# Two leading steps of a recurrent-attention and FFN kernel, regrouped as one batch with 256 tokens in 64-row tiles

## The chip, the cores and the metric

The kernel runs on one core of one Trainium2 chip. A core has engines that run side by side: TensorE (PE, matmuls; PEld is its weight load), VectorE (DVE), ScalarE (ACT), GpSimd (POOL) and SyncE (SP), and 16 DMA engines that all of them share. Each engine works through its own list of instructions in order; semaphores hold one engine back for another. The metric is device time in microseconds of the whole program, lower is better. The profile is of one execution on the chip.

## What is computed

A gated linear recurrence over 768 tokens (4 batches, 8 heads of 48), and after it a feed-forward network with a ReLU gate over all 3072 token rows:

```python
f = 1.0 / (1.0 + np.exp(-f_logit))
for t in range(S):
    state = f[:, :, t, :, None] * state + np.einsum('bhd,bhe->bhde', k[:, :, t], v[:, :, t])
    y[:, :, t] = np.einsum('bhd,bhde->bhe', q[:, :, t], state)
x = y.transpose(0, 2, 1, 3).reshape(B * S, H * D)          # 3072 x 384
gate = np.maximum(x @ w_gate, 0.0)                         # 384 x 1536
out = (gate * (x @ w_val)) @ w_out                         # 1536 x 384
```

## The kernel before

Time is cut into six steps of 128 tokens; a step takes all four batches, so 512 token rows. For a step, the attention makes a block `xT` (three times 128 features by 512 rows), and the FFN works on that block.

Attention of one batch in one step: f is turned into minus the log of the gate (ACT: Exp, then Ln, to `bneg`); a matmul with a triangle of ones sums it over the tokens ("cum"); ACT takes exponentials of both signs; k and q times these are the "hats" (`hats`); both are transposed to `qkT`; scores are k-hats by q-hats, one matmul for each head; DVE multiplies them by a triangular mask into `ptm`; the "rows" matmuls (`ps<-ptm,vpad` and `ps<-qkT,st`) add `ptm` times v and q-hats times the state to y; k-hats times v ("state", `ps<-vpad,hats`) go to the new state (`new_state`: one product in step 0, else a sum on DVE to `ssum` and a product on POOL to `st`). v is spread to `vpad` by POOL.

Three ways of transposing are in use. In steps 1 and 2 PE transposes the hats and DVE copies them (`pe_hats`, lines 687 to 700). From step 3 on the crossbar of the DMA does it (line 702, issued by SP). y comes out of PE already transposed where `x_way` is "tiled" (steps 0 to 2, 32-column tiles); else it comes out in natural order (lines 763 to 773) and the crossbar transposes it (line 795).

Step 0 is special (`twos = (0,)`, `attention_pair`). Two batches are taken together: each partition holds two neighbouring tokens of one batch, partitions 0 to 63 one batch and 64 to 127 the other, so that a DMA packet of f, k and q has two tokens, 384 bytes, instead of one token's 192. v is loaded in the plain way. The sum over tokens then needs two matrices (`upto`, `below`), and the transposes are written interleaved so that tokens come in order. As k-hats in token order are needed once more for the state, four more transposes a batch and a copy bring them back (`attention_back`, lines 623 to 637).

FFN (`ffn_hidden`, `ffn_out`): for each of 12 slices j of the hidden dimension, three matmuls for the gate (line 834), ReLU on ACT (840), three for the value (834 too), product on DVE to `gT` (844); then 12 matmuls for each batch with `wo` (877), ACT copies (887), SP stores (891). For a part of the slices, given by `halves`, the matmuls of two batches (256 columns) are done apart, so that the FFN can start with half of a block.

The order of work is not written by hand. Each operation is given to a planner (`Plan`) with an engine, an estimated duration and a priority; it lays all engines' lists out, picks PSUM banks by groups with limits, and puts in the semaphore waits. Written by hand is the order of the first DMAs, the string `first`: items run in this order on SP (inputs) and on POOL (weights: "wg0", "wv0" are thirds of the two first matrices); what follows an "@" is a load that must have landed first. In `link`, an operation named both in `after` (such a gate) and in `follows` (the predecessor in the same chain) keeps the second kind, which sets only the order.

```python
first = ("f0.0 k0.0 q0.0 v0.0 f0.1 k0.1 q0.1 v0.1 wg0@f0.1 wv0 wg1@q0.1 wv1 wg2 wv2 f1.0@wv1 k1.0 q1.0 v1.0 wo0@q1.0 wo1 wo2 "
         "f1.1 k1.1 q1.1 v1.1").split()
```

"f1.0" is f of step 1, first pair of batches. Until 15 us of the plan, PE is fed matmuls of zeros (lines 929 and 938) in its gaps.

Of the kernel before, what the change touches and what calls it, by code (L numbers as in the profile page):

```python
# [299 lines left out]
def bass_hgrn2_outer__then__ffn_reglu_kernel(  # L300
# [10 lines left out]
    twos = (0,)  # L311
    pe_hats = {(1, 0), (1, 1), (2, 0), (2, 1)}
    halves = {0: 6, 1: 6, 2: 6}
    x_way = {(c, pr): "tiled" if c < 3 else "xbar" for c in range(6) for pr in range(2)}
    s_twin = {(c, pr) for c in range(6) for pr in range(2)} - {(0, 0), (1, 0)}
    y_twin = {(1, 1), (2, 0), (2, 1)}
    flight = 3
    wsteps = 3
    first = ("f0.0 k0.0 q0.0 v0.0 f0.1 k0.1 q0.1 v0.1 wg0@f0.1 wv0 wg1@q0.1 wv1 wg2 wv2 f1.0@wv1 k1.0 q1.0 v1.0 wo0@q1.0 wo1 wo2 "
             "f1.1 k1.1 q1.1 v1.1").split()  # L320
# [32 lines left out]
    dec = [sb(f"dec{i}", [128, B, NP, 2], F32) for i in range(NA)]  # L353
# [20 lines left out]
    pick2 = sb("pick2", [128, 2], BF16)  # L374
    ident = sb("ident", [128, 128], BF16)
# [4 lines left out]
    pl = Plan({"bc": 2, "bc4": 4, "tp": 2, "s": 4, "y": 2, "kv": 1, "f": 4})  # L380
# [28 lines left out]
    def triangle(t, name, base, prio):  # L409
# [9 lines left out]
                                         pattern=[[0, 64], [1, 2]], channel_multiplier=-1), ["pick"], ["pick"], occ=0.3, prio=-20)  # L419
# [10 lines left out]
    add("DVE", lambda: ve.tensor_copy(pick2[:], same.ap[:, 0:2]), [same], ["pick2"], occ=0.1, prio=-19)  # L430
# [8 lines left out]
    for i in range(NA):  # L439
        fill("DVE", f"dec{i}", dec[i][:], 0.0, 32, -14)  # L440
# [20 lines left out]
    def load(n, c, b0, b1, after=()):  # L461
        last = tails.get("load")
        t = ld[n]
        both = c in twos and n != "v"
        if both:
            src = bass.AP(tensor=srcs[n].tensor, offset=b0 * H * S * D + c * C * D,
                          ap=[[2 * D, C // 2], [S * D, 2 * H], [1, 2 * D]])
            dst = bass.AP(tensor=t, offset=slot_of(n, c, b0 // 2) * 2 * HD, ap=[[NL[n] * 2 * HD, 128], [2 * D, H], [1, 2 * D]])
        else:
            src = bass.AP(tensor=srcs[n].tensor, offset=b0 * H * S * D + c * C * D,  # L470
                          ap=[[D, C], [S * D, (b1 - b0) * H], [1, D]])
            dst = t[:, slot_of(n, c, b0 // 2), :, :, :].rearrange("p b h d -> p (b h) d")
        op = add("SP", lambda: sy.dma_start(dst, src), [], in_keys(n, c, b0, b1),  # L473
                 occ=0.7 if both else 1.0, lat=0.9, prio=c * 100, after=after,
                 follows=[last] if last else [])
        tails["load"] = op
        dma(op, f"{n}{slot_of(n, c, b0 // 2)}", 0.95 * (b1 - b0), (64, 19, 27) if both else (128, 13.5, 23))
# [21 lines left out]
    loads, done = [], {}  # L499
    for item in first:  # L500
        item, _, behind = item.partition("@")
        gate = [done[behind]] if behind else []
        if item[0] == "w":
            op = load_w(item[:2], int(item[2:]), gate)
        else:
            c, pr = (int(x) for x in item[1:].split("."))
            op = load(item[0], c, 2 * pr, 2 * pr + 2, gate)
        done[item] = op
        if item[0] != "w":
            loads.append(op)  # L510

    def chain(line, *args, **kw):

        last = tails.get(line)
        tails[line] = add(*args, follows=[last] if last else [], **kw)
        return tails[line]
# [10 lines left out]
    def tokens(c, b, x, p, lo=0, hi=128):  # L527
        qi = (c * B + b) % NQ
        if c not in twos:
            return qkT[lo:hi, qi, x, p, :]  # L530
        row, two = NQ * 2 * NP * C, b % 2
        return bass.AP(tensor=qkT, offset=lo * row + (qi - two) * 2 * NP * C + x * 2 * NP * C + p * 2 * C + two,
                       ap=[[row, hi - lo], [2, C]])
# [18 lines left out]
    def attention_pair(c, b0):  # L552
# [3 lines left out]
        raw = {n: ld[n][:, slot_of(n, c, pr), :, :, :].rearrange("p b h d -> p (b h d)") for n in "fkq"}  # L556
        by_i = {n: raw[n].rearrange("p (h i d) -> p i h d", h=H, i=2) for n in "fkq"}
        key = {n: in_keys(n, c, b0, b0 + 2) for n in "fkq"}
        bi, e0, q0, ai = (w0 // 2) % NB, w0 % NE, w0 % NQ, c % NA
# [5 lines left out]
            follows=tails.pop("first q", []), **act_t(2 * HD))  # L565
        heads = lambda b_: b_.ap[:, 0:HD].rearrange("p (h d) -> p h d", h=H)
        for i in range(2):
            bc, ek = Bank("bc4"), Bank("bc4")

            def cum(i=i, bc=bc):  # L570
                for o in range(2):
# [3 lines left out]
            ex = expo[:, e0 + i, 0, :]  # L575
            add("ACT", lambda bc=bc, ek=ek: sc.activation(ek.ap[:, 0:HD], bc.ap[:, 0:HD], AF.Exp, scale=1.0),
                [bc], [ek], prio=P + 2 + i, opens=[ek], **act_t(HD))
            eqk = bc if i else f"expq{e0}_0"
            add("ACT", lambda bc=bc, i=i, ex=ex: sc.activation(bc.ap[:, 0:HD] if i else ex, bc.ap[:, 0:HD], AF.Exp, scale=-1.0),
                [bc], [eqk], prio=P + 2 + i, **act_t(HD))  # L580
            e, hi = ("DVE" if i else "POOL"), his[i]
            hk_op = add("DVE", lambda i=i, hi=hi, ek=ek: ve.tensor_tensor(hats[:, hi, 1, :, 0:D], by_i["k"][:, i], heads(ek), ALU.mult),
                        key["k"] + [ek, f"hats{hi}"], hk_(hi), prio=P + 2 + i, **dve_t(HD))
            add(e, lambda e=e, i=i, hi=hi, bc=bc, ex=ex: engine[e].tensor_tensor(
                hats[:, hi, 0, :, 0:D], by_i["q"][:, i], heads(bc) if i else ex.rearrange("p (h d) -> p h d", h=H), ALU.mult),
                key["q"] + [eqk, f"hats{hi}"], hq_(hi), prio=P + 3 + i, follows=[hk_op] if i else [], **elem_t(e, HD))
# [9 lines left out]
        for j in range(2):  # L596
            lo = 64 * j
            add("ACT", lambda lo=lo, j=j: sc.activation(
                dec[ai][lo:lo + 64, b0:b0 + 2, :, j].rearrange("p b n -> p n b"),
                tot.ap[lo:lo + 64, 0:2 * NP].rearrange("p (n b) -> p n b", n=NP), AF.Exp, scale=-1.0),  # L600
                [tot, f"dec{ai}"], [f"dec{ai}_{b}{j}{hh}" for b in (b0, b0 + 1) for hh in range(2)], prio=P + 10, **act_t(8))
        for x in (1, 0):
            tp = Bank("tp")

            def transposes(x=x, tp=tp):
                t16 = tp.ap[:, :].bitcast(BF16)
                for p in range(NP):
                    for i in range(2):
                        mm = te.transpose(t16[:, 2 * C * p:2 * C * (p + 1)].rearrange("q (r i b) -> q r i b", i=2, b=2)[:, :, i, :],
# [5 lines left out]
            e = "DVE" if x else "ACT"  # L615
            op = add(e, (lambda tp=tp, dst=dst: sc.activation(dst, tp.ap[:, :].bitcast(BF16), AF.Copy)) if e == "ACT"  # L616
# [3 lines left out]
            if not x and b0 == 0:  # L620
                tails["first q"] = [op]

    def attention_back(c, b, behind):
        w = c * B + b
        hi, qi = w % NH, w % NQ
        tp = Bank("tp")

        def transposes():
            t16 = tp.ap[:, :].bitcast(BF16)
            for p in range(NP):  # L630
                mm = te.transpose(t16[:, p * C:(p + 1) * C], tokens(c, b, 1, p), ident[:])
            return mm
        P = w * 10
        tails["transposes"] = add("PE", transposes, ["ident", f"qkT{qi}_10", f"qkT{qi}_11"], [tp], occ=0.3, lat=PE_L, prio=P + 30,
                                  opens=[tp], follows=[behind, tails["transposes"]])
        add("DVE", lambda: ve.tensor_copy(hats[:, hi, 1, :, :].rearrange("p h d -> p (h d)"), tp.ap[:, :].bitcast(BF16)[:, 0:4 * C]),
            [tp], hk_(hi), prio=P + 31, follows=[behind], **dve_t(256))

    def attention_front(c, b):
# [32 lines left out]
        if c < NC - 1:  # L672
            for j in range(2):
# [9 lines left out]
        add("POOL", lambda: gp.tensor_tensor(hq, qin[:, b % 2, :, :], ex[:, 0, :].rearrange("p (h d) -> p h d", h=H),  # L683
                                             ALU.mult),
# [344 lines left out]
```

## Time and profile before

| | us |
|---|---|
| median of 3 runs | 195.69 (195.66 to 196.28) |
| the profiled execution: its own time | 195.26 |
| its span, first to last instruction | 193.5 |
| first FFN matmul starts | 16.58 |
| PE busy from 16.58 to 191.2 | 171.2 of 174.6 |
| step 0's first f lands | 4.61 |
| step 1's first f issued, landed | 22.64, 28.85 |
| last step's last row matmuls start | 153.16 |

The granted TensorE clock was full throughout. In the profile's first part, each engine has its busy time, its share of the span and its instructions. In the second the span is cut into 40 slices of 4.84 us; a digit is the busy share in tenths. A line of a timeline gives start and duration in us, engine, line of the program, operation and operands, and in brackets for how long the engine had been idle and what ended it. PE's durations overlap, since matmuls are pipelined: the distance between starts is what a group costs. A line of the DMA queues gives packets, megabytes and share of 16 engines' time; q1 is SP's queue, q0 POOL's.

### The profile page before, as it was taken

To read this page: it belongs to the slowest core of one execution; us is meant where nothing else is said; L and a number is where in the kernel's file an instruction comes from. 1 tells how busy PE (TensorE), PEld (TensorE's weight loads), DVE (VectorE), ACT (ScalarE), POOL (GpSimd) and SP (SyncE) were. 2 spreads that over 40 slices of the span, in tenths; PEclk is the share of its full clock that TensorE was granted. 3 is DMA by queue.
4 is the path that set the end of the run, shared out by engine and by line. 5 is a ranking of instruction groups with operands and counts; after the bars stand their busy time and mean duration, and the time that the engine had idled before them with its cause. 6 is when DMAs were issued, how large, how long until landed. Compare 5 with 4: busy or idle time off the path is not lost.

```text
span 193.5 us, 4448 instructions
## 1 busy us (share of the span) xinstructions
PE 184.2 (95%) x1773; PEld 110.7 (57%) x1790; DVE 106.1 (55%) x195; ACT 111.0 (57%) x250; POOL 75.9 (39%) x108
## 2 busy tenths in 40 slices
PE   6986898999999999999999999999999999999995
PEld 1445694465788556767755544554555555544564
DVE  7756884671668878354776643743635622443300
ACT  3777439763596779838757758377343544244322
POOL 8377002958275949783533471634230000000000
PEclk9999999999999999999999999999999999999999
DMA  4999999999898999999796998998954220111113
GB/s 131 276 283 207 206 201 207 207 199 239 199 244 167 202 201 192 231 193 247 161 192 132 194 207 172 221 226 170 204 87 106 64 61 0 41 41 44 41 43 119
DMA packets 118196, 31.74 MB, mean 164 GB/s; under 512 B 111136, under 2 KB 118176, under 8 KB 118176
## 3 DMA queue, kind: packets, MB, share of 16 engines
q1 hardware_dynamic: 114192, 27.93, 68.1%
q0 software_dynamic: 3984, 3.54, 11.4%
q8 instruction: 14, 0.23, 0.5%
q14 instruction: 6, 0.05, 0.1%
HBM read 25.95 MB, written 4.72 MB: 158 GB/s over the span
## 4 chain that ended last, share of the span: by engine, by line
PE 70%; DMA 16%; SPq 5%; ACT 2%; DVE 2%; POOL 2%; issue 1%
PE ps L834 36%; PE ps L877 23%; DMA q_in<-in_q_dram 6%; DMA wv<-in_moe_w_val_dram 5%; SPq L473 4%; DMA f_in<-in_f_logit_dram 3%; DMA v_in<-in_v_dram 3%; PE ps L724 2%; PE ps L658 2%; PE ps L694 2%; PE ps L759 1%; PE ps L810 1%; DVE ptm L734 1%; PE ps L857 1%; POOL hats L683 1%
## 5 line engine op out<-in xcount | busy, mean ns | idle before, releaser
L844 DVE TENSOR_TENSOR gT<-relu,ps 128x512 bf16<-128x512 bf16 (+1 forms) x90 | 51.2, 578 | 53.9 <-PE ps L834 38.8
L834 PE MATMUL ps<-xT,wv 128*128 128x512 bf16 (+1 forms) x263 | 60.2, 336 | 1.8 <-DMA wv<-in_moe_w_val_dram 1.3
L840 ACT ACTIVATE relu<-ps 128x512 bf16<-128x512 f32 (+1 forms) x90 | 45.3, 511 | 27.6 <-PE ps L834 27.0
L834 PE MATMUL ps<-xT,wg 128*128 128x512 bf16 (+1 forms) x261 | 59.6, 335 | 0.9 <-ACT relu L840 0.5
L877 PE MATMUL ps<-wo,gT 128*128 128x384 bf16 x276 | 49.5, 326 | 0.1
L877 PEld LDWEIGHTS ps<-wo,gT 128*128 128x128 bf16 x276 | 25.9, 98 | 17.2
L834 PEld LDWEIGHTS ps<-xT,wv 128*128 128x128 bf16 x270 | 24.6, 98 | 19.4 <-DMA wv<-in_moe_w_val_dram 1.7
L834 PEld LDWEIGHTS ps<-xT,wg 128*128 128x128 bf16 x270 | 25.2, 98 | 17.9 <-ACT relu L840 0.4
L734 DVE TENSOR_TENSOR ptm<-ps,tri 128x512 bf16<-128x512 f32 x48 | 30.5, 684 | 8.3 <-PE ps L724 8.2
L680 POOL TENSOR_TENSOR hats<-k_in,expo 128x384 bf16<-128x384 f32 x20 | 19.8, 1000 | 20.8 <-ACT expo L668 11.0
L887 ACT ACTIVATE osb<-ps 128x384 f32<-128x384 f32 x23 | 11.2, 489 | 26.1 <-PE ps L877 26.1
L683 POOL TENSOR_TENSOR hats<-q_in,expo 128x384 bf16<-128x384 f32 x20 | 19.8, 1000 | 6.5 <-DMA q_in<-in_q_dram 6.5
L549 POOL TENSOR_TENSOR st<-ssum,dec 128x384 bf16<-128x384 f32 x16 | 13.3, 830 | 15.7 <-DVE ssum L547 15.5
L649 ACT ACTIVATE f_in<-f_in 128x768 f32<-128x768 f32 x10 | 8.4, 843 | 12.1 <-DMA f_in<-in_f_logit_dram 12.1
L714 POOL CAST vpad<-v_in 128x384 bf16<-128x384 f32 x24 | 11.7, 505 | 3.2 <-DMA v_in<-in_v_dram 3.2
L547 DVE TENSOR_TENSOR ssum<-ps,st 128x384 f32<-128x384 f32 x16 | 8.8, 552 | 4.9 <-PE ps L810 4.9
L668 ACT ACTIVATE expo<-ps 128x384 f32<-128x384 f32 x20 | 9.9, 493 | 0.5 <-PE ps L661 0.3
L670 ACT ACTIVATE expo<-ps 128x384 f32<-128x384 f32 x20 | 9.9, 496 | 0.0
L699 DVE COPY qkT<-ps 128x1024 bf16<-128x1024 bf16 x8 | 5.5, 690 | 7.5 <-PE ps L694 7.4
L724 PEld LDWEIGHTS ps<-qkT 48*128 48x128 bf16 x192 | 5.4, 94 | 5.3 <-issue 1.9
L651 ACT ACTIVATE bneg<-f_in 128x768 bf16<-128x768 f32 x10 | 8.4, 836 | 0.0
L724 PE MATMUL ps<-qkT 48*128 48x128 bf16 x192 | 7.6, 217 | 0.6 <-ACT qkT L616 0.5
(76 smaller groups left out, 146.2 us busy)
## 6 DMA issues: line engine op xcount, KB each, us to landing
f_in<-in_f_logit_dram SPq DMA_DIRECT2D x12, 384.0 KB, 5.6
k_in<-in_k_dram SPq DMA_DIRECT2D x12, 384.0 KB, 4.9
q_in<-in_q_dram SPq DMA_DIRECT2D x12, 384.0 KB, 5.7
v_in<-in_v_dram SPq DMA_DIRECT2D x12, 384.0 KB, 5.3
out_dram<-osb SPq DMA_DIRECT2D x23, 192.0 KB, 2.4
wg<-in_moe_w_gate_dram POOLq DMA_DIRECT2D x3, 384.0 KB, 7.7
wv<-in_moe_w_val_dram POOLq DMA_DIRECT2D x3, 384.0 KB, 8.8
wo<-in_moe_w_out_dram POOLq DMA_DIRECT2D x3, 384.0 KB, 6.2
```

The lines of the kernel that those rows point to most:

```text
L549: add("POOL", lambda: gp.tensor_tensor(t4(s_new), t4(tmp), rate, ALU.mult), [key] + dk, [f"S{b}_{c % 2}"], prio=P + 8, **pool_t(HD))
L668: add("ACT", lambda: sc.activation(ex[:, 1, :], bc.ap[:, 0:HD], AF.Exp, scale=1.0), [bc], [f"expk{ei}"], prio=P + 1, **act_t(HD))
L680: add("POOL", lambda: gp.tensor_tensor(hk, kin[:, b % 2, :, :], ex[:, 1, :].rearrange("p (h d) -> p h d", h=H), ALU.mult), in_keys("k", c, ...
L683: add("POOL", lambda: gp.tensor_tensor(hq, qin[:, b % 2, :, :], ex[:, 0, :].rearrange("p (h d) -> p h d", h=H), ALU.mult), in_keys("q", c, ...
L714: add("POOL", lambda vin=vin, vout=vout: gp.tensor_copy(vout, vin.rearrange("p (n j) d -> p n j d", j=2)), in_keys("v", c, b, b + 1) + [f" ...
L724: mm = te.matmul(s[j].ap[:, p * C:(p + 1) * C], tokens(c, b, 1, p, lo, lo + D), tokens(c, b, 0, p, lo, lo + D))
L734: add("DVE", lambda mi=mi, j=j, s=s: ve.tensor_tensor(ptm[mi][:, j, :, :], s.ap[:, :].rearrange("p (n t) -> p n t", n=NP), mask, ALU.mult) ...
L834: mm = te.matmul(bank.ap[:, 0:n], wt[:, kt, j * 128:(j + 1) * 128], xT[xi][:, kt, n0:n1], start=(kt == 0), stop=(kt == NK - 1))
L840: add("ACT", lambda: sc.activation(relu[ri][:, 0:n], gate.ap[:, 0:n], AF.Relu), [gate], [f"relu{ri}"], prio=P, **act_t(n))
L844: add("DVE", lambda: ve.tensor_tensor(gT[gi][:, j, n0:n1], relu[ri][:, 0:n], val.ap[:, 0:n], ALU.mult), [val, f"relu{ri}"], [f"gT{gi}_{j}_ ...
L877: mm = te.matmul(o[b].ap[:, 0:DM], gT[gi][:, j, b * C:(b + 1) * C], wo[:, j, :], start=(j == 0), stop=(j == NJ - 1))
L887: add("ACT", lambda b=b, oi=oi: sc.activation(osb[oi][:, :], o[b].ap[:, 0:DM], AF.Copy), [o[b]], [f"osb{oi}"], prio=P, **act_t(DM))
```

## The change

`twos` becomes `(0, 1)`, and a pair is now one batch with 256 tokens: partitions 0 to 63 hold its tokens 0 to 127 and the others tokens 128 to 255, two neighbours a partition. "Step 0" is batches 0 and 1, "step 1" batches 2 and 3, each with 256 tokens; steps 2 to 5 are as before, four batches with 128 tokens. Item "f1.0" is now f of batch 2 (256 tokens). All four inputs of both steps are loaded with 384-byte packets.

In a pair, work of the two 128-token halves goes in 64-row tiles of PE, partitions 0 to 63 for the first half and 64 to 127 for the second: 32 scores matmuls of 64 by 128, 16 state matmuls and 64 row matmuls with 64 rows, then 12 row matmuls with the state after the first half, for the second half only. Masks for these come from three POOL products (`mask2`). `attention_back` goes away. Both copies of the transposed hats are DVE's now. `new_state` is called for both halves in a row. In step 1 the hats are multiplied by POOL, except those of q of its first pair (DVE, `on_dve`).

Beside this: `pe_hats` is empty, so step 2's hats are transposed by the crossbar; `x_way` is "tiled" for step 3 too; `s_twin` and `y_twin` change; `halves` takes 8 slices for step 0; the bank group "kv" may hold two banks; `first` is a new order. Stores of steps 0 and 1 write other rows.

```diff
-    twos = (0,)
-    pe_hats = {(1, 0), (1, 1), (2, 0), (2, 1)}
-    halves = {0: 6, 1: 6, 2: 6}
-    x_way = {(c, pr): "tiled" if c < 3 else "xbar" for c in range(6) for pr in range(2)}
-    s_twin = {(c, pr) for c in range(6) for pr in range(2)} - {(0, 0), (1, 0)}
-    y_twin = {(1, 1), (2, 0), (2, 1)}
+    twos = (0, 1)
+    pe_hats = set()
+    halves = {0: 8, 1: 6, 2: 6}
+    x_way = {(c, pr): "tiled" if c < 4 else "xbar" for c in range(6) for pr in range(2)}
+    s_twin = {(c, pr) for c in range(6) for pr in range(2)}
+    y_twin = {(2, 0), (2, 1), (3, 0), (3, 1)}
+    on_dve = {(1, 0, 0, 0), (1, 0, 0, 1)}
-    first = ("f0.0 k0.0 q0.0 v0.0 f0.1 k0.1 q0.1 v0.1 wg0@f0.1 wv0 wg1@q0.1 wv1 wg2 wv2 f1.0@wv1 k1.0 q1.0 v1.0 wo0@q1.0 wo1 wo2 "
-             "f1.1 k1.1 q1.1 v1.1").split()
+    first = ("f0.0 k0.0 q0.0 v0.0 f0.1 k0.1 q0.1 v0.1 wg0@v0.0 wv0 wg1@q0.1 wv1 wg2 wv2 f1.0@v0.1 wo2@wv0 k1.0 q1.0 wo0@q1.0"
+             " f1.1 v1.0 wo1 k1.1@v1.0 q1.1@f1.1 v1.1").split()
...
-    pl = Plan({"bc": 2, "bc4": 4, "tp": 2, "s": 4, "y": 2, "kv": 1, "f": 4})
+    pl = Plan({"bc": 2, "bc4": 4, "tp": 2, "s": 4, "y": 2, "kv": 2, "f": 4})
...
-            src = bass.AP(tensor=srcs[n].tensor, offset=b0 * H * S * D + c * C * D,
-                          ap=[[2 * D, C // 2], [S * D, 2 * H], [1, 2 * D]])
+            src = bass.AP(tensor=srcs[n].tensor, offset=(2 * c + b0 // 2) * H * S * D, ap=[[2 * D, C], [S * D, H], [1, 2 * D]])
...
+        def scores(its):
+            for i in its:
+                for p in range(NP):
+                    for j in range(2):
+                        for b in range(2):
+                            mm = te.matmul(s[i][j].ap[64 * b:64 * b + 64, p * C:(p + 1) * C],
+                                           tokens(c, b0 + b, 1, p, 64 * j, 64 * j + D, i), tokens(c, b0 + b, 0, p, 64 * j, 64 * j + D))
+            return mm
...
+        def state():
+            for p in range(NP):
+                for i in range(2):
+                    for b in range(2):
+                        mm = te.matmul(kv[b].ap[:, p * 96:(p + 1) * 96],
+                                       hats[64 * b:64 * b + 64, his[i], 1, 2 * p:2 * p + 2, :].rearrange("p h d -> p (h d)"),
+                                       bass.AP(tensor=vpad[vs[i]], offset=64 * b * VW + p * VSTEP, ap=[[VW, 64], [64, 2], [1, D]]),
+                                       start=(i == 0), stop=(i == 1), skip_group_check=True)
+            return mm
...
+        def rows():
+            todo = [(n, p, VSTEP * p + 32 * m + 16 * (m == 2), m // 2) for n, (p, m) in enumerate(blocks)]
+            todo += [(3 * p + 1, p, VSTEP * p + 48, 1) for p in range(NP)]
+            for i in range(2):
+                for at, (n, p, col, j) in enumerate(todo):
+                    lo = 32 * (n % 4)
+                    for b in range(2):
+                        mm = te.matmul(y[b].ap[lo:lo + 32, n // 4 * C:(n // 4 + 1) * C],
+                                       vpad[vs[i]][64 * b:64 * b + 64, col:col + 32], ptm[ms[i]][64 * b:64 * b + 64, j, p, :],
+                                       start=(i == 0 and at < 4), stop=(b == 0 and i == 1 and at >= 12), skip_group_check=True)
+            for n, (p, m) in enumerate(blocks):
+                lo = 32 * (n % 4)
+                mm = te.matmul(y[1].ap[lo:lo + 32, n // 4 * C:(n // 4 + 1) * C],
+                               st[bt][0][:, p * SSTEP + 32 * m:p * SSTEP + 32 * m + 32], tokens(c, b0 + 1, 0, p),
+                               start=False, stop=(n >= 8), skip_group_check=True)
+            return mm
```

In the built program, the changed first part of the lists stands as follows. ACT: f of batch 1 (Exp, Ln), three of its four hat exponentials, Exp of f of batch 2, the fourth hat exponential, two decays (`dec`), Ln of batch 2, both `xT` copies of batch 0, four hat exponentials of batch 2, the first ReLU. PE: all of batch 0's attention; cum and totals of batch 1; rows of batch 0; k transposes, state and q transposes of batch 1; cum and totals of batch 2; one FFN slice (gate, value); scores of batch 1; seven FFN groups; k transposes of batch 2; rows of batch 1; 13 FFN groups; q transposes of batch 2. SP: the sixteen loads of steps 0 and 1, of which only q of batch 3 has a wait (on f of batch 3). POOL: after batch 0's q product and v copies the thirds wg0, wv0, wg1 (wait on q of batch 1), wv1; v copies and q product of batch 1, a state product, wg2, wv2, wo2 (wait on wv0).

## What is predicted

> **What bounds the kernel now.** I read the page first: busy times, slices, chain of waits.
>
> ```profile
> PE 184.2 (95%) x1773; PEld 110.7 (57%) x1790; DVE 106.1 (55%) x195; ACT 111.0 (57%) x250; POOL 75.9 (39%) x108
> ...
> PE   6986898999999999999999999999999999999995
> ...
> PE 70%; DMA 16%; SPq 5%; ACT 2%; DVE 2%; POOL 2%; issue 1%
> ```
>
> PE is full from the seventh slice (29 us) on, and nothing else comes near. So the end is: when the FFN starts, plus PE work after that, plus PE's idle time. The chain in order of time shows the start:
>
> ```profile
> 7.80 4.96 DMA q_in<-in_q_dram
> 12.77 0.29 issue
> 13.06 0.77 POOL wg L493
> 13.82 8.80 DMA wv<-in_moe_w_val_dram
> 22.63 0.01 issue
> 22.64 6.21 DMA f_in<-in_f_logit_dram
> ```
>
> Step 0's inputs, then weights, then step 1's f, each strictly behind the other. PE's timeline shows what that costs:
>
> ```profile
> 16.58 0.49 PE L834 MATMUL ps<-xT,wg 128*128 128x256 bf16 x3
> ...
> 18.12 0.50 PE L834 MATMUL ps<-xT,wv 128*128 128x256 bf16 x3 [0.60 <-DMA wv<-in_moe_w_val_dram]
> ...
> 22.67 0.50 PE L834 MATMUL ps<-xT,wv 128*128 128x256 bf16 x3 [0.71 <-DMA wv<-in_moe_w_val_dram]
> ```
>
> The FFN starts at 16.6 us and is held twice by weights, 0.8 us each. The DMA queues come next, one microsecond each: 7 to 8 us (v, 192-byte packets), 9 to 10 (f, k, q, 384 bytes), 14 to 15 (weights alone), 42 to 43 (weights and loads together).
>
> ```profile
> q1 hardware_dynamic: 1335, 0.26, 125.7%
> ...
> q1 hardware_dynamic: 841, 0.32, 115.2%
> ...
> q0 software_dynamic: 201, 0.21, 123.3%
> ...
> q0 software_dynamic: 184, 0.14, 88.6%
> q1 hardware_dynamic: 218, 0.04, 36.8%
> ```
>
> A 384 KB load is 1024 packets of 384 bytes (1.22 us) or 2048 of 192 (1.53 us); a weight third is 384 packets (1.9 us). Beside weights a load falls to about 200 packets a microsecond.
>
> **The budget.** The last FFN matmul ends at 189.20 + 1.99 = 191.2. FFN matmuls: 432 of 512 columns (18 take 3.89 us, so 93.4) and 288 of 384 (12 take 1.95, so 46.8), 140.2 in all. Attention after 16.6, by the chain's pieces: a batch of steps 1 and 2 costs cum 0.26, eight transposes 0.45, scores 0.28, 28 row matmuls 0.45, state 0.17, so 1.61, eight of them 12.9; steps 3 and 4 (rows 0.37, no transposes) 1.08 x 8 = 8.6; step 5 0.82 x 4 = 3.3; what is left of step 0: transposes 0.45, scores 0.55, rows 0.68, transposes back 0.90, state 0.68 = 3.3. Sum 28.1. Idle is the rest: 191.2 - 16.6 - 140.2 - 28.1 = 6.3, of which about 2.1 before 30.5 us and 4.2 spread over the remaining 160.
>
> **What the Trainium skill says.** "DMA: Bandwidth & Descriptors", section "Queues, rings and completion order": each DMA engine takes the queues that have work in turn and switches only between packets. The trace agrees at 42 to 43 us (218 against 184); it doesn't show who goes first when weights arrive at a busy load queue. The same page, "Specifications", puts line rate at 512 bytes and more; the trace shows the direction (0.32 against 0.26 MB in a microsecond). "TensorEngine Tiling (Array Packing)", "Theoretical Speedup": up to twice for 64 rows. The 48-row scores show it partly: 16 matmuls of 128 columns in 0.55 us, 34 ns each, where eight 128-row transposes take 0.45, 56 each. "PSUM — Partial Sum Buffer", "Engine vs sequencer instructions": ACT, DVE and POOL are strict first-in first-out and matmuls keep their order. The trace agrees (at 16.13 transposes wait 0.5 us for a DVE hat, with all of PE behind), and the whole start rests on it.
>
> **Work removed and added on PE.** From the FFN's start on, the changed order still has: of batch 1 scores and rows; batch 2 without its cum; all of batch 3. Prices not in the trace: 32 scores matmuls cost 1.10 at 34 ns each, 0.55 if four tiles run together; I take 0.65. 16 state matmuls: 0.67 at 42 ns (4 take 0.17), 0.34 in pairs; I take 0.5. 64 + 12 row matmuls: 1.22 at 16 ns (28 take 0.45), 0.70 if the 64 run in pairs; I take 1.05. Then 0.65 + 1.05 = 1.7; transposes 0.9 + 0.65 + 0.5 + 1.05 = 3.1; and 4.1 with cum 0.65 and totals 0.35. Sum 8.9, ends -1.6 and +2.0. Step 2 loses four times eight transposes: 4 x 1.16 = 4.6. Step 3's tiled rows cost 0.45 for 0.37: 4 x 1.16 = 4.6. Step 4 4.3, step 5 3.3. Together 25.7 against 28.1, so 2.4 us less. The FFN's start and idle may thus sum to 16.6 + 6.3 + 2.4 = 25.3 before the change costs time.
>
> **The new start.** In the changed order the first FFN matmul stands behind the totals of batch 2. ACT's order puts step 1's first exponential (f of batch 2) ahead of batch 1's last hat exponential, and its Ln ahead of both xT copies of batch 0. So with L, the landing of that f: exp 0.84, exp 0.47, two decays 0.36, Ln 0.84 end at L + 2.5; two xT copies at L + 3.5; PE's cum (0.65) and totals (0.35) at L + 3.6. The FFN starts at L + 3.65.
>
> L: f 1.0 is written as gated on v 0.1, but the built order has no wait there (v 0.1 is also its predecessor, and that entry wins), so SP issues it at once. The hardware queue's packets begin at 2.8 and run 841 a microsecond: eight loads end at 12.5, a ninth alone at 13.7. The first weight DMA no longer waits for f 0.1 but follows POOL's two v copies, which end at 9.9, so it is issued 0.8 us sooner than at 10.7; its packets came 2.6 us after issue, so from 12.5. Before, they only thickened as the load queue drained, so I take full sharing from 13.2. By then f has 1024 - 0.7 x 841 = 435 packets left. A pair of a 384-byte and a 1024-byte packet takes 1/841 + 1/201 = 1/162 us: 2.7 us, packets end 15.9, landing at 16.5 with 0.6 for the end (f 0.0's from its packets); I take L = 16.3, ends 14.3 (not shared) and 20 (shared from 12.5, tails stretched). The FFN starts at 20.0, against 16.6.
>
> What cover is there? Weights: thirds of 2.4 us from 13.2 land at 16.3 and 18.7, so the FFN no longer waits for them. The first xT copies could have been ready by 17.4 (rows after the four masks, which end at 14.9, and 1.1 of matmuls); the rest is f's wait. PE's new idle from 17.1 to 20 shows in this sum as the later start, not in the idle term.
>
> **Stalls after it.** (a) DVE: batch 1's copies, two state operations and four masks (0.62 each) stand ahead of the first gT, and ACT's four exponentials of batch 2 ahead of the first ReLU. With four banks for gate and val, the fourth val waits: 1.3 us. (b) PE's transposes of batch 2's k wait for k 1.0: its packets end at 15.9 + 6.3 = 22.2, landed 22.9, two POOL hats of 1.0 to 24.9; PE is there at L + 8.5 = 24.8; with a gap between loads as at 39 to 40 us (55 load packets beside 257 of weights) up to 1.2 more: I take 0.8. (c) q 1.0 lands at 29.2, DVE hats 30.4; PE arrives at 31.1: hidden, 0.7 to spare. (d) The late 4.2 stay. Step 2's four crossbar transposes (L702, 1.3 us of SP each, 3.3 to landing) wait for POOL's hats on SP with later loads behind, but their scores stand more than 60 FFN groups (some 28 us) past the FFN's start in PE's order: nothing, at most +1. Step 3 takes four x transposes off SP, where loads waited behind them (93 to 95 us): nothing to -0.4. DVE loses eight copies of 0.69, in a stage that is PE's. Loads of ten inputs in half the packets save 0.3 us each of DMA, used in L.
>
> Sum: 20.0 + 1.3 + 0.8 + 4.2 = 26.3 against 25.3: +1.0 us. The profiled execution's own time is 195.26 (span 193.5 and 1.8 around it); the median of the runs shown is 195.69, 0.4 more. So 196.7.
>
> **Rivals.** (1) Faster: f 1.0 lands before weights share the engines. Place: the DMA queues at 13 us. If L is 14.3, the FFN waits for wv instead, 18.7 + 0.15: start 18.9; k 1.0 comes a microsecond sooner, so stall (b) goes: 18.9 + 1.3 + 4.2 = 24.4, -0.9, and with 64-row tiles in pairs down to -2.5; taken together 194.3. It decides below L = 15.3. For: weight packets thickened only when loads had drained. Against: 218 to 184 when both are queued. (2) Weights starve behind twelve loads: with the load queue never empty, wg starts only near 20 us and wv lands at 24; start 24, less stalls, 24 + 0.3 + 4.2 = 28.5, +3.2: 198.9. For: the same thickening. Against: 42 to 43 us. (3) The change moves the start by as much as it saves: 195.7.
>
> **Chances.** Forecast 0.40 (own range 196.3 to 198.2), rival 1 0.31, rival 2 0.13, rival 3 0.16. Under 0.3% (0.6 us) can't be told from no change. Faster 0.31, same 0.16, slower 0.53. The range 193.4 to 199.4 takes in rival 1 with cheap tiles and rival 2.
>
> **What would show it.** First FFN group near 20 us with ACT's f exponential ending in a wait for f_in just before; the k transposes of batch 2 released by POOL's hats at about 25; 76 row matmuls in about 1.05 us; no idle on wv. Wrong if the FFN starts before 19 or after 22, if the tiles run at the full 34, 42 and 16 ns, or if PE shows more than 5 us of idle past 45 us.

## The result and the profile after

| | median, us | lowest to highest | ratio to before, 95% interval |
|---|---|---|---|
| before, 4 runs | 195.68 | 195.15 to 196.28 | |
| after, 4 runs | 220.3 | 219.69 to 224.0 | 1.1247, 1.1194 to 1.1299 |

The change costs 24.6 us. The forecast was 196.7 us, +1 us, with a range up to 199.4: the direction was right and the size was not. Ratios here leave out runs that lie over 1.5% above the fastest of their kernel (six of 20 are left of the run with rows alone, below), so a median over all runs can be above what its ratio says. The profiled execution took 220.69 us, its span 218.9.

The page of the kernel after: TensorE's busy time, then its slices, its granted clock and the DMA engines' slices (40 slices of 5.47 us).

```profile
PE 191.6 (88%) x2042; PEld 114.3 (52%) x2042; DVE 105.2 (48%) x193; ACT 110.0 (50%) x246; POOL 74.7 (34%) x109
...
PE   7965999999479399986395599999999999999995
...
PEclk9998899999969889999979799999999999999999
DMA  6999999934599799995748999978995321000013
```

The DMA engines' slices of the kernel before (4.84 us each):

```profile
DMA  4999999999898999999796998998954220111113
```

Before, TensorE was full from the seventh slice on. Now it is full from the fifth slice up to 55 us, has holes up to 126 us, and is full again to the end. It is idle for 27.3 us (218.9 less 191.6) against 9.3 before, and it is busy for 7.4 us more. 18.0 and 7.4 are the 25.4 us by which the span grew. The 7.4 us go with the clock, which is at half speed for 17.1 us in all, in five stretches of 3.41 us; the same instructions, in an execution at full clock (the run with rows alone, below), were busy for 184.1 us. After the eighth slice the DMA engines, full in the kernel before, fall to 0.3 to 0.5 just ahead of the first hole.

What TensorE waits for between 45 and 140 us, first in the kernel before and then in the kernel after (who waited, for whom: us in total, times, longest):

```profile
PE ps L810 <- POOL vpad L714: 0.6, 2, 0.4
```

```profile
PE ps L883 <- POOL vpad L790: 8.2, 2, 4.4
PE ps L800 <- DMA qkT<-hats: 8.0, 2, 4.6
PE ps L800 <- issue: 2.7, 1, 2.7
PE ps L734 <- ACT bneg L727: 0.3, 1, 0.3
```

GpSimd's copies of v come late because v landed late, and the crossbar transposes land late too: everything that is late comes out of SP's queue. That queue after, from 46 to 66 us (start, us that the issue took, what it issued):

```profile
46.91 1.26 SPq L963 DMA_DIRECT2D out_dram<-osb  x2
48.22 1.46 SPq L483 DMA_DIRECT2D q_in<-in_q_dram  x1
49.72 7.72 SPq L483 DMA_DIRECT2D v_in<-in_v_dram  x1
57.48 1.46 SPq L483 DMA_DIRECT2D f_in<-in_f_logit_dram  x1
...
63.23 1.07 SPq L963 DMA_DIRECT2D out_dram<-osb  x2
64.35 5.82 SPq L778 DMA_TRANSPOSE qkT<-hats  x1
```

Two stores, and the second load behind them is held for 7.72 us (its issue alone takes SP that long); two more, and the transpose behind them is held for 5.82. In the kernel before, none of the three issues behind the same two stores takes longer than 2.1 us:

```profile
46.44 1.21 SPq L891 DMA_DIRECT2D out_dram<-osb  x2
47.69 1.15 SPq L473 DMA_DIRECT2D k_in<-in_k_dram  x1
48.89 2.08 SPq L473 DMA_DIRECT2D q_in<-in_q_dram  x1
51.01 1.45 SPq L473 DMA_DIRECT2D v_in<-in_v_dram  x1
```

What the DMA engines did meanwhile, 54 to 56 us, before and then after (queue: packets, MB, their time as a share of 16 engines):

```profile
q1 hardware_dynamic: 1795, 0.59, 118.6%
```

```profile
DMA packets 66, 0.11 MB, mean 54 GB/s; under 512 B 0, under 2 KB 65, under 8 KB 65
...
q1 hardware_dynamic: 65, 0.10, 13.2%
```

Here is the cause in one line: in two microseconds 65 packets of 1536 bytes on SP's queue, about 50 GB/s, and 13.2% of the time of sixteen engines, which is that of two. On this queue packets of that size are stores, here those of step 0. The change writes them with the DRAM pattern of 2 by 64 rows, and its outermost dimension is 2. A store has 128 such packets; at 32.5 a microsecond it takes 3.9 us, and the eight stores of steps 0 and 1 take 31 us. The Trainium skill, "DMA: Bandwidth & Descriptors", section "Why a DMA increments its semaphore by 16 and not by 1", says how many engines a transfer gets: the largest number up to 16 that divides the slowest dimension over 1 of both sides. Sides of 2 and 128 give 2, which agrees with the 13.2%.

Loads behind such stores come late: q, issued at 48.22 us, landed after 10.9 us, and v after 11.3. A load here is 2048 packets of 192 bytes. From 48 to 54 us 1808 packets of that kind moved, about 14 sixteenths of one load (1792), and from 54 to 57 us none. That fits a load spread over sixteen engines whose part on two of them stands behind the stores. The traces do not show single engines, so this step is inferred.

Three theories were put to the test. **T1**: the two-engine stores are the loss. **T2**: step 2's crossbar transposes hold SP's queue, whatever the stores do. **T3**: the new start, with loads beside the weights, costs more than the forecast has.

### The profile page after: what moved, and what is told of

The parts are those of the page before. It is cut to its first block, busy times and chain, and to the rows that moved or that the text cites. A ratio compares the mean times of both kernels' runs of the same rounds, so it can differ in the third digit from the quotient of the medians.

```text
span 218.9 us, 4982 instructions
## 1 busy us (share of the span) xinstructions
PE 191.6 (88%) x2042; PEld 114.3 (52%) x2042; DVE 105.2 (48%) x193; ACT 110.0 (50%) x246; POOL 74.7 (34%) x109
## 4 chain that ended last, share of the span: by engine, by line
PE 62%; DMA 23%; SPq 7%; POOL 3%; ACT 3%; issue 1%
PE ps L905 36%; PE ps L948 17%; DMA qkT<-hats 8%; DMA k_in<-in_k_dram 6%; SPq L483 5%; DMA q_in<-in_q_dram 5%; DMA v_in<-in_v_dram 4%; PE ps L800 2%; SPq L778 1%; PE ps L928 1%; POOL hats L605 1%; POOL hats L760 1%; PE ps L883 1%; PE ps L835 1%; PE ps L847 1%
## 5 line engine op out<-in xcount | busy, mean ns | idle before, releaser
L905 PE MATMUL ps<-xT,wv 128*128 128x512 bf16 (+1 forms) x276 | 65.5, 349 | 0.0
L905 PE MATMUL ps<-xT,wg 128*128 128x512 bf16 (+1 forms) x276 | 65.4, 349 | 0.1
L810 DVE TENSOR_TENSOR ptm<-ps,tri 128x512 bf16<-128x512 f32 x32 | 20.5, 684 | 21.1 <-PE ps L800 21.1
L760 POOL TENSOR_TENSOR hats<-q_in,expo 128x384 bf16<-128x384 f32 x16 | 15.8, 995 | 28.9 <-DMA q_in<-in_q_dram 28.9
L756 POOL TENSOR_TENSOR hats<-k_in,expo 128x384 bf16<-128x384 f32 x16 | 15.8, 995 | 23.5 <-ACT expo L744 13.5
L565 POOL TENSOR_TENSOR st<-ssum,dec 128x384 bf16<-128x384 f32 x16 | 13.2, 828 | 14.5 <-DVE ssum L563 14.5
L883 PE MATMUL ps<-vpad,hats 128*128 128x96 bf16 x48 | 4.2, 219 | 8.2 <-POOL vpad L790 8.2
L666 DVE TENSOR_TENSOR ptm<-ps,mask 128x512 bf16<-128x512 f32 x16 | 9.9, 682 | 1.9 <-PE ps L657 1.9
L790 POOL CAST vpad<-v_in 128x384 bf16<-128x384 f32 x16 | 7.8, 504 | 5.5 <-DMA v_in<-in_v_dram 5.5
L744 ACT ACTIVATE expo<-ps 128x384 f32<-128x384 f32 x16 | 7.8, 490 | 2.3 <-PE ps L737 2.0
L883 PEld LDWEIGHTS ps<-vpad,hats 128*128 128x128 bf16 x48 | 3.0, 104 | 9.7 <-POOL vpad L790 8.7
L746 ACT ACTIVATE expo<-ps 128x384 f32<-128x384 f32 x16 | 7.9, 495 | 0.0
## 6 DMA issues: line engine op xcount, KB each, us to landing
wg<-in_moe_w_gate_dram POOLq DMA_DIRECT2D x3, 384.0 KB, 10.2
```

The source lines that it names most:

```text
L565: add("POOL", lambda: gp.tensor_tensor(t4(s_new), t4(tmp), rate, ALU.mult), [key] + dk, [f"S{b}_{c % 2}"], prio=P + 8, **pool_t(HD))
L666: add("DVE", lambda i=i, j=j, mask=mask: ve.tensor_tensor(ptm[ms[i]][:, j, :, :], s[i][j].ap[:, :].rearrange("p (n t) -> p n t", n=NP), ma ...
L756: add("POOL", lambda: gp.tensor_tensor(hk, kin[:, b % 2, :, :], ex[:, 1, :].rearrange("p (h d) -> p h d", h=H), ALU.mult), in_keys("k", c, ...
L760: add(e, lambda: engine[e].tensor_tensor(hq, qin[:, b % 2, :, :], ex[:, 0, :].rearrange("p (h d) -> p h d", h=H), ALU.mult), in_keys("q", ...
L810: add("DVE", lambda mi=mi, j=j, s=s: ve.tensor_tensor(ptm[mi][:, j, :, :], s.ap[:, :].rearrange("p (n t) -> p n t", n=NP), mask, ALU.mult) ...
L905: mm = te.matmul(bank.ap[:, 0:n], wt[:, kt, j * 128:(j + 1) * 128], xT[xi][:, kt, n0:n1], start=(kt == 0), stop=(kt == NK - 1))
```

## Experiments: the stores and the crossbar

**Stores in two transfers of 64 rows.** The rows that a transfer writes still lie two rows apart; only the outermost dimension becomes 64 on both sides. Every other engine's order is as in the kernel after.

```diff
-  both = [(bass.AP(..., offset=at, ap=([[DM, 2], [2 * DM, 64]] ...
+  both = [(bass.AP(..., offset=at + i * DM, ap=[[2 * DM, 64], [1, DM]]), osb[oi][64 * i:64 * i + 64, :])
+          for i in range(2)] if g in twos else ...
```

> The changed kernel, each store of steps 0 and 1 cut into two transfers of 64 partitions and 64 rows (row distance 2 rows), so that the outermost dimension of both sides is 64 and not 2; every other engine's order unchanged. T1 (a store whose outermost dimension is 2 goes through 2 of the 16 DMA engines, 3.9 us each, and SP's queue stands behind it): 196 to 198 us, the loads and crossbar transposes of 47 to 75 us land within 2 to 4 us of issue, TensorE idle past 45 us down from about 25 us to under 6. T2 (step 2's hats by crossbar hold SP's queue whatever the stores do): 214 or more. T3 (the new start is what costs): 217 or more, since nothing of it is touched.

Measured: 202.82 us beside 197.04 before (ratio 1.0259, 1.0167 to 1.0352). Most of the loss is gone, so it was not the distance of the rows; but about 5 us more than T1 allows for are left.

**Step 2's hats on TensorE again**, stores as in the kernel after: `pe_hats = {(2, 0), (2, 1)}`.

> The changed kernel with its stores as they are, and step 2's hats turned by TensorE again as in the kernel before. T1 (stores through two engines): the loads still wait, 210 to 220 us; the 8 us wait for the crossbar transpose at about 67 us goes, the waits for q_in and k_in stay. T2 (crossbar transposes of step 2 hold SP): 195 to 199.

Measured: 225.5 us, ratio 1.1355 (1.1243 to 1.1467). That is over T1's range too, but T2 falls: without step 2's crossbar transposes the kernel is no faster.

**Both edits.**

> Both edits: stores of steps 0 and 1 in two transfers of 64 rows, and step 2's hats on TensorE again. T1: within 1.5 us of the run with the stores alone (196 to 198). T2: the two edits add up, this is 195 to 198 and the run with the stores alone is well above 205. The difference of the two runs is the price of step 2's crossbar transposes, which the prediction put at 0 to +1 us.

Measured: 206.0 us, ratio 1.0349 (1.0238 to 1.046), 3.2 us more than with the stores alone, and outside what T1 and T2 had; the intervals overlap. In the profile of this run an f of step 1 landed late (below) and TensorE waited 6.4 us at the start, so the difference says little of step 2. The forecast's price for the crossbar transposes, nothing to +1 us, isn't contradicted.

**The two-engine stores alone, put into the kernel before.** Bytes, instructions and their order are those of the kernel before; rows within a block of 128 land in another order than the output asks for.

```diff
-  both = [(bass.AP(tensor=out.tensor, offset=at, ap=[[DM, C], [1, DM]]), osb[oi][:, :])]
+  both = [(bass.AP(tensor=out.tensor, offset=at, ap=([[DM, 2], [2 * DM, 64]] if g < 2 else [[DM, C]]) + [[1, DM]]), osb[oi][:, :])]
```

> The kernel before with one edit: the rows that steps 0 and 1 store go to DRAM in the order of the changed kernel's pattern (2 times 64 rows at a distance of 2 rows), so that rows within a block of 128 are written in another order; all instructions and their order are otherwise the same. T1 (the two-engine store alone is the cost): 207 to 220 us, stores of about 3.9 us each, loads of 45 to 75 us landing 5 to 10 us late. T2 and T3: 195.7 within 1 us, since hats and start are those of before.

Measured: 222.55 us, ratio 1.1305 (1.1223 to 1.1388), so +25.5 us, a little over the range that T1 gave. Its DMA engines from 54 to 56 us, and its queue (as above):

```profile
q1 hardware_dynamic: 75, 0.10, 13.7%
```

```profile
48.44 1.41 SPq L891 DMA_DIRECT2D out_dram<-osb  x2
49.89 1.43 SPq L473 DMA_DIRECT2D k_in<-in_k_dram  x1
51.37 7.76 SPq L473 DMA_DIRECT2D q_in<-in_q_dram  x1
...
60.93 2.02 SPq L891 DMA_DIRECT2D out_dram<-osb  x2
62.99 0.93 SPq L473 DMA_DIRECT2D f_in<-in_f_logit_dram  x1
63.96 8.11 SPq L473 DMA_DIRECT2D k_in<-in_k_dram  x1
```

The same rate, the same 8 us holds behind each pair of stores, in a kernel with the old start and the old hats. The pattern of eight stores is by itself worth what the whole change lost.

## Experiments: what was left

**ScalarE's Exp of step 1's first f put behind** the second batch's hat exponentials and the first batch's copies of x, on top of the stores in two.

```diff
-  add("ACT", lambda: sc.activation(raw["f"], raw["f"], AF.Exp, scale=-1.0), key["f"], key["f"], prio=P, ...
+  add("ACT", lambda: sc.activation(raw["f"], raw["f"], AF.Exp, scale=-1.0), key["f"], key["f"], prio=P, follows=first_act ...
```

The reason to try it was this line of ScalarE's timeline, first of the kernel after, then of the run with both edits (in brackets: idle before, and for what):

```profile
17.24 0.84 ACT L580 ACTIVATE f_in<-f_in 128x768 f32<-128x768 f32 x1 [3.33 <-DMA f_in<-in_f_logit_dram]
```

```profile
21.96 0.84 ACT L580 ACTIVATE f_in<-f_in 128x768 f32<-128x768 f32 x1 [8.35 <-DMA f_in<-in_f_logit_dram]
```

The same f landed at 17.2 in one execution and at 22.0 in another, with the same first loads in the same order; in the run with the stores alone it was there before ScalarE asked, at 14.03.

> The changed kernel with the stores in two transfers of 64 rows, and in ScalarE's order the Exp of step 1's first f put behind the second batch's last hat Exp and the first batch's two copies of x, so that the landing of that f no longer holds these. T3 (part of what is left after the stores is the new start, whose length hangs on when that f lands): the stall before the second batch's q transposes (2.4 to 6.4 us in the profiles so far) goes to under 0.5, FFN starts near 18, the time is 198 to 201 and the runs lie within 1.5 us of each other. T2 (what is left is step 2's crossbar transposes in SP's queue): no gain in the median beyond 1 us over the run with the stores alone (202.8), idle at 85 to 140 us unchanged at about 4 us.

Measured: 200.33 us, 199.18 to 201.08, beside 195.70 (1.0247, 1.0184 to 1.031). As a ratio that is no gain over the stores alone; the runs lie closer together, within 1.9 us. The wait before the second batch's q transposes was 0.9 us where under 0.5 was expected. The FFN began at 17.3 us, then waited 1.63 us for wv.

**On top of it, three variants**: step 2's hats on TensorE; step 3's x by crossbar (`"tiled" if c < 3`); `flight = 4`.

> As the run with the Exp put behind, and step 2's hats turned by TensorE again: 4 crossbar transposes fewer in SP's queue at 55 to 85 us. T2: 2 to 5 us less than that run, TensorE idle at 85 to 140 us down to under 2 us. T3: within 1 us of it.

Measured: 202.61 us (1.0339, 1.0262 to 1.0416): 2.3 us more by the medians, where T2 had 2 to 5 us less. The intervals overlap.

> As the run with the Exp put behind, and step 3's x through the crossbar as in the kernel before: 4 crossbar transposes more in SP's queue, 0.1 us per batch less on TensorE. If queue time on SP is what the loads of steps 3 and 4 lack (T2), 1 to 3 us slower than that run; if not, equal within 0.7 us (the prediction gave this edit 0 to -0.4 us).

Measured: 206.52 us (1.0559, 1.049 to 1.0628): 6.2 us slower, twice the top of what was expected. The edit puts four more transposes into SP's queue, and makes step 3's rows on TensorE a little cheaper. In the profile the waits of TensorE from 45 us on come to 8.0 us where those of the run with the Exp behind come to 3.6, and its clock is at half speed from 111 to 122 us, where that run has full speed.

> As the run with the Exp put behind, and a load may be issued when the fourth load before it has landed instead of the third. If the loads of step 2 are late because they are issued late (the DMA engines carry 93 GB/s at 45 to 50 us in the run with the stores alone), the lull at 42 to 50 us shrinks and the time falls by 1 to 3 us; if DMA capacity is the limit, no change within 1 us.

Measured: 199.29 us (1.0226, 1.0149 to 1.0304): 1.0 us less, with intervals that overlap, so this settles nothing.

**x written in the order of DRAM's rows**, so that each store is one transfer of 128 rows again, with the order of TensorE, VectorE and GpSimd unchanged. The permutation moves into a copy that ScalarE makes anyway:

```diff
-  dst = xT[xi][:, :, (b0 + b) * C:(b0 + b + 1) * C]
-  src = lambda b=b: y[b].ap[:, 0:HD].rearrange("p (n t) -> p n t", n=NK)
+  dst = xT[xi][:, :, (b0 + b) * C:(b0 + b + 1) * C].rearrange("p n (t i) -> p n i t", i=2)
+  src = lambda b=b: y[b].ap[:, 0:HD].rearrange("p (n i t) -> p n i t", n=NK, i=2)
...
+  both = [(bass.AP(tensor=out.tensor, offset=at, ap=[[DM, C], [1, DM]]), osb[oi][:, :])]
```

> As the run with the Exp put behind, but ScalarE's copies of x in steps 0 and 1 write the 128 columns in the order of DRAM's rows (two tokens a partition side by side), so that each store of these steps is again one transfer of 128 rows, as in the kernel before; the order of TensorE, VectorE and GpSimd is the same. If the eight extra store issues in SP's queue (0.6 to 1.5 us each) are what the loads of steps 2 and 3 wait for, 1 to 3 us less than that run (200.3); if not, equal within 0.7 us, or up to 1 us more if ScalarE's strided copies are dearer than 0.49 us.

Measured: 196.21 us over 12 runs, beside 196.25 (1.0011, 0.9965 to 1.0056): 4 us less than with the stores in two, where 1 to 3 were expected. The copy costs 0.60 us (0.49 before), and nobody waits for it. SP's queue shows where time went, first in the run with the Exp behind and the stores in two, then in this one:

```profile
58.05 3.84 SPq L963 DMA_DIRECT2D out_dram<-osb  x4
61.94 1.34 SPq L778 DMA_TRANSPOSE qkT<-hats  x1
63.33 0.58 SPq L483 DMA_DIRECT2D q_in<-in_q_dram  x1
```

```profile
58.21 1.06 SPq L963 DMA_DIRECT2D out_dram<-osb  x2
59.32 1.31 SPq L778 DMA_TRANSPOSE qkT<-hats  x1
60.68 0.58 SPq L483 DMA_DIRECT2D q_in<-in_q_dram  x1
```

Four issues take 3.84 us where two take 1.06, and q is asked for 2.65 us later. With one transfer for each store no wait of TensorE is listed from 45 us to the end; with two it was 3.6 us in all.

**That edit alone on the kernel after**; the order of TensorE, VectorE and GpSimd is that of the kernel after.

> The changed kernel with one thing undone: its copies of x in steps 0 and 1 write the columns in the order of DRAM's rows, so that the stores of these steps are single transfers of 128 rows; the order of all engines is that of the changed kernel. T1: the whole excess over the forecast is the stores, 195.5 to 199 us, no TensorE idle between 45 and 140 us beyond 1 us; against the run that also puts the Exp behind (196.2) the difference is the price of the start's Exp, 0 to 2 us. If more than the stores costs late in the kernel: over 200.

Measured: 197.85 us median, 194.19 to 204.08 over 20 runs, beside 196.14; ratio 0.9998 (0.9955 to 1.0041). The page's TensorE slices, and then TensorE's waits from 45 us on:

```profile
PE   7978779999999999999999999999999999999995
```

```profile
PE ps L734 <- ACT bneg L727: 1.1, 3, 0.6
```

With one pattern repaired the late holes are gone, and the time is near the forecast. By the median of all runs it is 1.7 us above the kernel before, by the mean 2.2 (198.53 beside 196.29). Its runs spread over 10 us, where those with the Exp behind spread over 3.6 (194.8 to 198.43). That the landing of f makes this spread is argued from the two ScalarE lines above; no long run of this kernel was profiled.

**The first loads as in the kernel before** (step 1's loads start when the second part of wv has landed), with rows in order and the Exp behind. The gate of the first weights and the place of wo go back too, so it is the start as a whole that is compared.

```diff
-  first = (... wg0@v0.0 wv0 wg1@q0.1 wv1 wg2 wv2 f1.0@v0.1 wo2@wv0 k1.0 q1.0 ...
+  first = (... wg0@f0.1 wv0 wg1@q0.1 wv1 wg2 wv2 f1.0@wv1 k1.0 q1.0 v1.0 ...
```

> As the run with rows in order, and the first loads in the order and with the gates of the kernel before: step 1's loads start when the second part of wv has landed, not beside the weights. T3 (loads beside the weights delay wg and wv, TensorE idles 1.5 to 2.5 us, its clock drops to 0.6 for some 4 us): FFN starts at 16.5 to 17.5 instead of 18 to 20, no drop of the clock at 20 to 25 us, 2 to 4 us less than the run with rows in order. If the prediction's gain of early loads were real, it would be slower by 1 us or more.

Measured: 193.48 us over 20 runs beside 196.25 (0.989, 0.9858 to 0.9922). It is 2.7 us faster than with loads beside the weights, and faster than both kernels. The FFN begins at 18.05 us, half a microsecond later than expected (the clock was at half speed from 14.5 to 17.9 us), but then it is not interrupted:

```profile
17.34 0.88 PE L632 MATMUL ps<-ident,hats 128*128 128x128 bf16 x8
18.05 0.49 PE L905 MATMUL ps<-xT,wg 128*128 128x256 bf16 x3
18.38 0.49 PE L905 MATMUL ps<-xT,wv 128*128 128x256 bf16 x3
```

With loads beside the weights the first group was at 17.50 and the second only at 19.72, released by wv, and the clock was down from 20.2 to 23.6. From the first FFN matmul to the last, TensorE now idles for 1.9 us instead of 4.2 and is busy for 168.8 instead of 170.4. Weights alone move about 205 packets a microsecond here, beside loads about 150. T3 holds for 2.7 us, though not for the 24.6: the early loads cost more than they bring.

**The same with step 1's loads one part of the weights earlier** (`f1.0@wv0`).

> As the run with rows in order and the start of the kernel before, but step 1's loads start one part of the weights earlier (when the first part of wv has landed and not the second). If the 1.8 us wait for the third batch's hats at 30 to 40 us is on the path, 0.5 to 1.5 us less than that run (193.5); if the loads then starve wg and wv again, TensorE waits for wv reappear and it is 0.5 to 2 us more.

Measured: 195.49 us over 20 runs beside 196.14 (0.9973, 0.9944 to 1.0003). Slower by 2 us than the later gate, by the medians; the wait for wv is back, with 0.4 us, and the rest of the order moved too, so what makes the 2 us is open.

## Why the prediction was wrong

**The step that failed is the list of parts itself.** The forecast prices the start, the tiles, the transposes and the loads, and then "(d) The late 4.2 stay". It has no term for the eight stores of steps 0 and 1, though the change says that they write other rows. The term was worth 22.5 to 25.5 us: putting the two-engine stores alone into the kernel before cost 25.5; repairing them alone in the kernel after took it from 220.3 to a median of 197.85. That such a pattern gets two engines could have been had beforehand from the page of the Trainium skill cited above; its section "Rules for kernel authors" has the rule as advice too, to put a size that is a multiple of 16 outermost. "Wrong if ... PE shows more than 5 us of idle past 45 us" was the condition that came true: the waits listed after 45 us come to 19.2 us.

**L, the landing of f.** Forecast 16.3, ends 14.3 and 20; 17.2 in the profile after, and the FFN began at 20.57, forecast 20.0. In profiles of other kernels with the same first loads f landed by 14.0 (two profiles) and at 17.8, 18.7 and 22.0, a spread wider than the forecast's ends. It goes with the start of the weights: by 13 us none of their packets had moved in the profiles with 14.0 and 17.2, 20 in that with 17.8, 26 with 18.7 and 86 with 22.0. What makes the weights start earlier is open. The sharing itself was forecast well: 162 pairs of packets a microsecond, 157 measured from 20 to 21 us. Where f landed by 14.0, rival (1) came about: the FFN started at 18.1 and 18.3 and then waited for wv. Rival (2), weights that start only near 20 us, is in no profile.

**Stall (a)**, 1.3 us for VectorE and four banks: no such wait is listed. In its place the clock fell. TensorE's timeline of the kernel after, start and length of FFN groups of three matmuls:

```profile
22.96 0.82 PE L905 MATMUL ps<-xT,wg 128*128 128x256 bf16 x3
23.57 0.66 PE L905 MATMUL ps<-xT,wv 128*128 128x256 bf16 x3
24.07 0.49 PE L905 MATMUL ps<-xT,wg 128*128 128x256 bf16 x3
24.40 0.49 PE L905 MATMUL ps<-xT,wv 128*128 128x256 bf16 x3
```

0.61 us from start to start, then 0.33. From 20.57 to 24.07 there are four groups and 32 scores matmuls; at full speed they take 4 x 0.33 + 0.57 = 1.9 us instead of 3.5. So 1.6 us are lost, but to the clock.

**Stall (b)**, the k transposes waiting for GpSimd's hats: forecast 0.8 us at 24.8; 0.32 at 26.19 after, and 2.20 at 25.32 in the run with rows alone, where f had landed early and rival (1) had this stall go. The mechanism is right, the size is not. **(c)** hidden: right, the q transposes at 31.96 had no wait.

**Matmul prices.** Of the kernel after, from start to start:

```profile
34.14 0.64 PE L657 MATMUL ps<-qkT 48*64 48x128 bf16 x32
34.71 0.50 PE L905 MATMUL ps<-xT,wv 128*128 128x256 bf16 x3
...
45.09 0.52 PE L675 MATMUL ps<-vpad,hats 64*128 64x96 bf16 x16
45.53 1.47 PE L948 MATMUL ps<-wo,gT 128*128 128x384 bf16 x8
46.94 0.74 PE L695 MATMUL ps<-ptm,vpad 64*32 64x128 bf16 x64
47.60 0.35 PE L700 MATMUL ps<-qkT,st 128*32 128x128 bf16 x12
47.89 0.62 PE L632 MATMUL ps<-ident,hats 128*128 128x128 bf16 x8
```

Scores 0.57 (forecast 0.65), state 0.44 (0.5), 76 rows 0.95 (1.05). All are a little cheaper. A matmul costs 18, 28 and 10 ns in the 64-row tiles, where the forecast had 34, 42 and 16 for one at a time, so the gain is 1.5 to 1.9 times; the 12 matmuls with the state take 24 ns each where the forecast had 16.

**Step 2's crossbar transposes**, nothing to +1: not contradicted. **Step 3's x in tiles**, nothing to -0.4: undersized. It was worth 6.2 us with the stores in two; its price with single stores was not measured.

**The sum** of everything but the stores came to 196.7; the kernel with the stores repaired has a median of 197.85, and with the Exp behind 196.21. Its terms can be held against the profile with rows alone (195.33 us, clock full), from the first FFN matmul to the last. Before, the FFN started at 16.58, and TensorE was busy for 171.2 us and idle for 3.4; here it starts at 18.29 and is busy for 168.8 and idle for 4.1. The work shrank by 2.4 us, as forecast. The start is 1.7 us later where 3.4 was forecast, and the idle time is 0.7 us more where no more was forecast. That the sum comes near is partly luck, since these two errors have opposite signs, and where f landed at 17.2 the clock's 1.6 us came on top.

The forecast's idle time of 6.3 us in the kernel before was a remainder of its budget. The profile has 3.4 (174.6 less 171.2), and 1.6 of it after 30.5 us, where (d) put 4.2; the rest is matmul time that the budget's prices missed. It stood on both sides of the sum and so did no harm.

## What to carry to other kernels

When a change regroups tokens over partitions, list every DMA whose access pattern changes, stores included, and read the outermost dimension of each: a 2 there means two engines, 3.9 us for 192 KB, and on a shared queue everything behind it is late. Put a permutation into a copy that an engine with time to spare makes anyway (0.11 us more each here) rather than into the DMA, and don't split the DMA either if its queue is the one that feeds the kernel (4 us here). Loads started beside the weights that the next stage waits for take these weights' bandwidth; the start without them was 2.7 us better here.

## What had not been expected of the hardware

Two stores in the queue did not go to different engines: 65 packets in 2 us is the rate with a pair of them issued, about 50 GB/s for both, and the other traffic of the queue stood still.

TensorE's clock fell to 0.66 on average at 20 to 25 us after an idle time of 2.43 us, and for 3.4 us after 1.63 us in the run with the Exp behind, but not at all after 2.54 us in the run with the stores alone. All twelve profiles of kernels with the new attention have the same gap of 1.44 us just before 15 us; in five of them the clock is at half speed within 2 us of it, in seven it stays full there. The Trainium skill, "TensorE: Matmul & The Clock Gate", section "What's actually happening", gives an idle window of about 3.4 us for the fall to half speed; here it also fell after shorter gaps, though not after each, and what decides is not shown.

How long a fall lasts can be read from the traces. Cut into windows of half a microsecond, they show the granted clock at full or half speed, with values between only at the edges of a fall. Each time it was at half for 3.41 us (eleven times, in the kernel after and five others) or two, three or four times that (6.8, 10.2 and 13.7 us). So an estimate from these lengths: a wait on TensorE can cost, on top of itself, up to 1.7 us of work (half of 3.41) for each such stretch.
